# Gated delta attention and two MLPs: first loads, a solve moved one step earlier, and the second product two pairs behind

## The chip, the core and the metric

The kernel runs on one core of a Trainium2 chip. The metric is the device time of one execution in microseconds; all times here are in microseconds. A core has five engines that each run their own instructions in order: TensorE (PE in the rows; PEld are its weight loads), VectorE (DVE), ScalarE (ACT), GpSimd (POOL) and SyncE (SP, which here only issues DMA transfers). They wait for one another by semaphores.

## What is computed

Three parts run one after another; the output of each is the input of the next.

```python
# 1: attention with a state, per head, for t in 0..767 (4 batches, 8 heads, head dim 48)
k_n = k / (norm(k) + 1e-06)
y[t] = q[t] @ state
state += beta[t] * outer(k_n[t], v[t] - k_n[t] @ state)
# 2: 3072 tokens, 384 -> 2048 -> 384
h = maximum(x @ w_in, 0);  x = (h * h) @ w_out
# 3: 384 -> 768 -> 384
x = maximum(maximum(x @ w1, x @ w2), x @ w3) @ w_out2
```

The weights of parts 2 and 3 come as float64.

## The kernel before

**Chunks and systems.** The sequence is cut into 12 chunks of 64 positions, which are the 12 steps of the first two parts. Within a chunk the recurrence becomes a triangular system. `kkps` (L166) makes its matrix: K times K transposed (kk, L160, copied from PSUM by ScalarE at L175) and the masked product P with the queries (L176), two halves per chunk, stored to DRAM. `start32` (L252) loads kk again in another layout, M, with two chunks side by side on the 128 partitions (L262); `prep` (L222) copies the diagonal to ss (L224) and computes norms, a square root on ScalarE (L194) among them; `solve` (L238) eliminates with 61 VectorE instructions (L243, L245, L246); `finish32` stores the result xt (L278), which `attention` loads as xb. A solve so serves two chunks: `HALVED[g]` are chunks 2g and 2g+1.

**Attention of a chunk** (`attention`, L321) is a chain of small steps over two halves p (16 of the 32 batch-head pairs each): transposed blocks xT (L340), products pZ and pW, values scaled by the norms (`st0`, L361), `mm_u` (pU, L382), `st2` (pY, L395; the new state Sb, L404), `st3` (transposition pT, then xh, the high part on ScalarE, L419, and xl, the low part on VectorE, L420).

**First MLP of a chunk** (`moe_a`, L434). float32 operands are split in a high and a low part, and each product takes three matmuls. 16 blocks of 128 hidden units are taken in 8 pairs. For a pair, `s1` is 18 matmuls (L446), then ScalarE makes relu (L451), square (L452) and the high part gh (L453), VectorE the low part gl (L454), and `s2` is 18 matmuls with them (L465). The code runs s1 one pair ahead of s2. At the end, two copies xs (L476) leave for DRAM.

**Weights.** `convert` (L81) loads raw float64 bits (L87) and makes the two parts: an absolute value on ScalarE (L90), bit operations on VectorE (L93 to L98), the high part on ScalarE (L99), the low part on VectorE (L100). There are 16 pieces of w_in in the prologue, the first NE = 5 ahead of the first solve; 16 of w_out (8 in the prologue's end, the others in step 0); 12 of the second MLP's first weights in steps 9 to 11.

**Order.** The prologue makes kk of chunks 0 and 1, the first solve, attention(0) and w_in. Then `steps` (L480) runs twelve times moe_a(c) with other generators beside it, each advanced at its rate: attention(c + 1), kkps for a later pair of chunks and solve32 by the tables `KK` and `SOLVE` (step: pair of chunks). The code gives only an order of priority: a scheduler of the framework decides the final order on each engine, and extra order can be forced with `behind(i, j)`, which puts instruction i after j. Buffers of kk and P are pieces of two large tiles, big and buf, and in the prologue ksr. After the steps the second MLP runs (L637, L654).

## Time and profile before

| | us |
|---|---|
| median of 3 runs | 1062.96 (1060.36 to 1063.26) |
| the profiled execution | 1065.6 |
| its span | 1063.9 |
| PE busy | 933.4 (88%) |
| VectorE busy | 477.6 (45%) |
| ScalarE busy | 395.1 (37%) |
| chain that ended last | PE 73%, DVE 10%, DMA 10%, issue 3% |

The span is the time between the first and the last instruction of the profiled execution; the rest of its time lies around it. The chain that ended last is followed back from the last instruction, at each step to what released it. Step c begins here with the first matmul of moe_a(c) that reads xl: 111.1, 169.5, 243.9, 293.6, 350.5, 399.5, 458.1, 505.0, 562.2, 619.4, 671.2 and 716.2; the second MLP begins at 757.9.

### The profile page before, as it was taken

Reading aid. Unit: us, or ns where it says so; the run is one execution under the profiler, and the core shown is the slowest. Engines: PE = TensorE matmul, PEld = TensorE weight load, DVE = VectorE, ACT = ScalarE, POOL = GpSimd, SP = SyncE. Lnnn points to the kernel's source line nnn. Section 1 sums busy time; section 2 is a strip of 40 time slices with the busy share of each in tenths; the row PEclk is TensorE's granted clock in tenths of the full one; section 3 lists DMA queues with packets and bytes.
Section 4 is the critical chain, followed back from the end, with each engine's and each line's share of the span. In section 5 each row is a group of like instructions: output and inputs, shape, how many; then the busy total and the mean of one; then the engine's idle time right before and its main releaser. Section 6 shows DMA issues by size and latency. Waiting matters only on the chain.

```text
span 1063.9 us, 26753 instructions
## 1 busy us (share of the span) xinstructions
PE 933.4 (88%) x11706; PEld 856.9 (81%) x11706; DVE 477.6 (45%) x1057; ACT 395.1 (37%) x780; POOL 125.6 (12%) x200
## 2 busy tenths in 40 slices
PE   4004999959998999899988989998999999999998
PEld 4004898948997999799988979998888888888887
DVE  2799937547223841384257641227352323232221
ACT  2126653423443444344454444455431212121111
POOL 1323010130202020202020202000110000000000
PEclk8555898978999899999998989998999999999999
DMA  9954562552245134514452341104220100000001
GB/s 265 291 122 119 174 177 75 139 139 49 73 128 158 49 95 118 159 53 105 116 165 85 82 144 59 34 9 127 89 75 15 45 16 30 15 16 23 8 23 38
DMA packets 89333, 98.44 MB, mean 93 GB/s; under 512 B 49120, under 2 KB 66784, under 8 KB 89216
## 3 DMA queue, kind: packets, MB, share of 16 engines
q1 hardware_dynamic: 74624, 59.36, 20.3%
q0 software_dynamic: 10496, 31.60, 10.1%
q10 hardware_dynamic: 4096, 5.77, 1.6%
q8 instruction: 92, 1.51, 0.6%
q14 instruction: 25, 0.20, 0.1%
HBM read 71.53 MB, written 25.17 MB: 91 GB/s over the span
## 4 chain that ended last, share of the span: by engine, by line
PE 73%; DVE 10%; DMA 10%; issue 3%; ACT 3%; SPq 1%; POOL 1%; DVEq 0%; ACTq 0%; POOLq 0%
PE p L637 21%; PE p L446 17%; PE px L465 17%; PE po L654 7%; DMA buf<-kk 2%; PE pU L382 2%; DMA kk<-big 2%; DVE buf L243 2%; DVE buf L245 2%; DMA raw<-in_moe_w_dram 2%; PE pk L160 1%; PE pW L354 1%; PE pY L395 1%; PE pZ L344 1%; PE pA L372 1%
## 5 line engine op out<-in xcount | busy, mean ns | idle before, releaser
L465 PE MATMUL px<-gh,wout 128*128 128x256 f32 x1152 | 227.3, 296 | 22.3 <-ACT gh L453 22.3
L465 PEld LDWEIGHTS px<-gh,wout 128*128 128x128 f32 x1152 | 187.0, 200 | 26.2 <-ACT gh L453 23.6
L637 PE MATMUL p<-x_h,w 128*128 128x512 f32 x648 | 203.4, 395 | 0.0
L465 PE MATMUL px<-gl,wout 128*128 128x256 f32 x576 | 170.3, 296 | 5.9 <-DVE gl L454 5.8
L446 PE MATMUL p<-xh,win_h 128*128 128x256 f32 x576 | 169.9, 296 | 0.2
L446 PE MATMUL p<-xl,win_h 128*128 128x256 f32 x576 | 167.3, 294 | 0.0
L446 PE MATMUL p<-xh,win_l 128*128 128x256 f32 x576 | 166.3, 289 | 0.0
L454 DVE TENSOR_TENSOR gl<-p,gh 128x512 fp32r<-128x512 f32 x96 | 65.9, 687 | 175.9 <-ACT gh L453 175.4
L637 PEld LDWEIGHTS p<-x_h,w 128*128 128x128 f32 x648 | 121.6, 188 | 27.1
L637 PE MATMUL p<-x_l,w 128*128 128x512 f32 x324 | 128.1, 395 | 0.0
L451 ACT ACTIVATE gg<-p 128x512 f32<-128x512 f32 x96 | 57.1, 596 | 190.8 <-PE p L446 188.4
L465 PEld LDWEIGHTS px<-gl,wout 128*128 128x128 f32 x576 | 115.3, 200 | 8.4 <-DVE gl L454 7.9
L446 PEld LDWEIGHTS p<-xh,win_h 128*128 128x128 f32 x576 | 114.8, 199 | 1.9 <-ACT xh L419 0.7
L446 PEld LDWEIGHTS p<-xh,win_l 128*128 128x128 f32 x576 | 114.6, 199 | 0.0
L446 PEld LDWEIGHTS p<-xl,win_h 128*128 128x128 f32 x576 | 113.2, 198 | 1.6
L643 DVE TENSOR_TENSOR mx<-p,mx 128x512 f32<-128x512 f32 x36 | 24.9, 691 | 137.1 <-PE p L637 137.1
L637 PEld LDWEIGHTS p<-x_l,w 128*128 128x128 f32 x324 | 61.0, 188 | 14.6
L645 ACT CAST hh<-mx 128x512 fp32r<-128x512 f32 x36 | 22.3, 620 | 130.8 <-DVE mx L644 130.8
L245 DVE TENSOR_TENSOR buf<-buf 128x30 f32<-128x30 f32 (+9 forms) x180 | 59.5, 330 | 5.2
L243 DVE TENSOR_TENSOR buf<-buf 128x30 f32<-128x30 f32 (+9 forms) x180 | 59.2, 329 | 5.4
L452 ACT ACTIVATE p<-gg 128x512 f32<-128x512 f32 x96 | 57.6, 601 | 2.7
L453 ACT CAST gh<-p 128x512 fp32r<-128x512 f32 x96 | 56.1, 585 | 2.7
(132 smaller groups left out, 1362.0 us busy)
## 6 DMA issues: line engine op xcount, KB each, us to landing
kq<-in_kc_dram POOLq DMA_DIRECT2D x22, 448.0 KB, 4.1
raw<-in_moe_w_dram SPq DMA_DIRECT2D x18, 384.0 KB, 4.4
p<-p POOLq DMA_DIRECT2D x24, 256.0 KB, 3.3
raw<-in_moe_w_out_dram SPq DMA_DIRECT2D x13, 384.0 KB, 3.7
buf<-in_kc_dram SPq DMA_DIRECT2D x11, 448.0 KB, 3.8
big<-in_kc_dram SPq DMA_DIRECT2D x11, 448.0 KB, 4.3
v<-in_vt_dram POOLq DMA_DIRECT2D x24, 192.0 KB, 3.9
ktp<-in_kt_dram POOLq DMA_DIRECT2D x24, 192.0 KB, 3.4
```

The lines of the kernel that those rows point to most:

```text
L243: eng.tensor_tensor(out=tv, in0=M[:, 0:j, j].unsqueeze(2).broadcast_to([u, j, m]), in1=M[:, j, j + 1:n].unsqueeze(1).broadcast_to([u, j, m ...
L245: yield eng.tensor_tensor(out=M[:, 0:j, j + 1:n], in0=M[:, 0:j, j + 1:n], in1=tv, op=ALU.add)
L446: pe.matmul(p1[:, j], w[:, k, f], x[c][:, k], start=n == 0 and j == 0, stop=n == 8, skip_group_check=True)
L451: act.activation(out=gg, in_=p1, func=AF.Relu)
L452: act.activation(out=p1, in_=gg, func=AF.Square)
L453: act.copy(gh, p1)
L454: vec.tensor_sub(out=gl, in0=p1, in1=gh.bitcast(F32))
L465: pe.matmul(acc[m], w, x[:, j], start=f == 0 and i == 0 and m != 1, stop=f == NF - 1 and i == 2, skip_group_check=True)
L637: pe.matmul(p, w[i][:, k, fs], x[:, k], start=n == 0, stop=n == 8)
L643: vec.tensor_max(out=t, in0=ps[1], in1=t)
L645: act.copy(hh[:, f], t2)
L654: pe.matmul(po[:, 0:DM], x[:, f, js], w[:, f], start=i == 0, stop=i == 17)
```

## The change

1. **The start.** Four pieces of w_in instead of five are loaded first. The kk stores go out from SP instead of ScalarE; the stores of P of chunks 0 and 1 are later, on POOL. M of chunk 0 is loaded from POOL and of chunk 1 from SP. All other raw loads come behind the last load of M (`raw_after[:] = loaded`), and ss comes behind the fourth conversion (`prep_after`). The stores of xt go out from ScalarE and POOL.
2. **Chunk 0.** attention(0) takes both halves through each of its steps side by side, with tiles of their own.
3. **Chunks 2 and 3.** Their kk is made in the prologue, the mask product behind the first solve, instead of in step 0; their solve stands in step 0, behind the eighth conversion of w_out, instead of in step 1. attention(2) is no longer put off by 11 turns.
4. **The lag.** s2 stands two pairs behind s1 instead of one; relu works in place in PSUM, and gh and gl have three buffers.
5. **Second MLP's weights.** VectorE's part of the conversions in step 9 comes behind the last gl of step 8.

```diff
+LAG = 2
...
-        lo_eng.tensor_tensor(out=lo, in0=l.bitcast(F32), in1=hi.bitcast(F32), op=ALU.subtract)
+        parted.append(lo_eng.tensor_tensor(out=lo, in0=l.bitcast(F32), in1=hi.bitcast(F32), op=ALU.subtract).ins)
...
-    def kk_store(c, p, kk, dma):
-        return [dma.dma_start(kk_d[c][:, t, U2 * p:U2 * p + U2], kk[64 * t:64 * t + 64]).ins for t in range(2)]
-
-    def kkps(cs, ps_, dma=nc.sync):
+    def kk_store(c, p, kk):
+        for t in range(2):
+            nc.sync.dma_start(kk_d[c][:, t, U2 * p:U2 * p + U2], kk[64 * t:64 * t + 64])
+
+    def kkps(cs, ps_, late_p=None):
...
+            for i in mul_after:
+                behind(kk_ends[1], i)
             yield
-            stores = kk_store(c, p, ks[:, 0], dma)
-            for t in range(2):
-                o = 64 * t
-                stores.append(nc.sync.dma_start(p_d[c][o:o + 64, U2 * p:U2 * p + U2], ks[64 - o:128 - o, 1]).ins)
-            p_stored[:] = stores[2:]
+            kk_store(c, p, ks[:, 0])
+
+            def p_store(dma, c=c, p=p, ks=ks):
+                return [dma.dma_start(p_d[c][64 * t:64 * t + 64, U2 * p:U2 * p + U2], ks[64 - 64 * t:128 - 64 * t, 1]).ins for t in range(2)]
+
+            if late_p is None:
+                p_store(nc.sync)
+            else:
+                late_p.append(p_store)
...
+        i = vec.tensor_copy(ss, diagonal(M, n))
+        for j in prep_after:
+            behind(i.ins, j)
...
-                dma.dma_start(M[o:o + 32], units(kk_d[c][..., 32 * s:32 * s + 32], 32 * s, 32))
+                loaded[0] = dmas[i].dma_start(M[o:o + 32], units(kk_d[c][..., 32 * s:32 * s + 32], 32 * s, 32)).ins
...
-        for fs in ((st0, 0),), ((zz, k21),), ((ww, 0),), ((mm_u, 0),), ((st2, 0),), ((st0, 1), (st3, 0)), ((mm_u, 1),), ((st2, 1),), ((st3, 1),):
+        if c:
+            order = ((st0, 0),), ((zz, k21),), ((ww, 0),), ((mm_u, 0),), ((st2, 0),), ((st0, 1), (st3, 0)), ((mm_u, 1),), ((st2, 1),), ((st3, 1),)
+        else:
+            order = ((st0, 0), (st0, 1)), ((zz, k21),), ((ww, 0),), ((mm_u, 0), (mm_u, 1)), ((st2, 0), (st2, 1)), ((st3, 0), (st3, 1))
+        for fs in order:
...
-            gg = gp.tile([128, 2, TB], F32, name="gg", tag="gg")
-            gh = gp.tile([128, 2, TB], F32R, name="gh", tag="gh")
-            gl = gp.tile([128, 2, TB], F32R, name="gl", tag="gl")
-            act.activation(out=gg, in_=p1, func=AF.Relu)
-            act.activation(out=p1, in_=gg, func=AF.Square)
+            gh = gp.tile([128, 2, TB], F32R, name="gh", tag="gh", bufs=LAG + 1)
+            gl = gp.tile([128, 2, TB], F32R, name="gl", tag="gl", bufs=LAG + 1)
+            act.activation(out=p1, in_=p1, func=AF.Relu)
+            act.activation(out=p1, in_=p1, func=AF.Square)
             act.copy(gh, p1)
-            vec.tensor_sub(out=gl, in0=p1, in1=gh.bitcast(F32))
+            last_gl[0] = vec.tensor_sub(out=gl, in0=p1, in1=gh.bitcast(F32)).ins
...
-            if fp:
-                s2(fp - 1)
+            if fp >= LAG:
+                s2(fp - LAG)
...
-        s2(NF // 2 - 1)
+        for fp in range(NF // 2 - LAG, NF // 2):
+            s2(fp)
+            if fp < NF // 2 - 1:
+                yield
         for i, n in enumerate((2, 1)):
-            xs = gp.tile([128, 2, TB], F32, name="xs", tag="gg")
+            xs = gp.tile([128, 2, TB], F32, name="xs", tag="xs", bufs=1)
...
+                for j in solve_after:
+                    behind(i.ins, j)
...
-        drain(kkps(HALVED[0], (p1, at), act))
-        NE = 5
-        raw_done = list(p_stored)
+        ps_stores = []
+        drain(kkps(HALVED[0], (p1, at), ps_stores))
+
+        NE = 4
         after[:], abs_after[:] = kk_ends[1:], kk_ends[0:1]
         for f in range(NE):
             load_win(f, vec, nc.sync)
-        raw_after[:] = raw_done
-        drain(solve32(0, pool))
-        x_after.append(selected[0])
-        drain(attention(0))
-        x_after.clear()
+        prep_after.append(parted[-1])
+        first_solve = solve32(0, (pool, nc.sync), (act, pool))
+        next(first_solve)
+        prep_after.clear()
+        raw_after[:] = loaded
+        stores = [i for f in ps_stores for i in f(pool)]
+        for i in stores:
+            behind(i, selected[0])
+        drain(first_solve)
+        solved.append(ops[-1])
+        x_after.append(stores[-1])
         after[:], abs_after[:] = ops[-1:], normed[0:1]
         for f in range(NE, NF):
             load_win(f, vec, nc.sync)
+
+        mul_after.append(solved[0])
+        kc_after.append(raws[-1])
+        drain(kkps(HALVED[1], (p1, at)))
+        mul_after.clear()
+        kc_after.clear()
+        drain(attention(0))
...
-        KK, SOLVE = {0: 1, 1: 2, 3: 3, 5: 4, 7: 5}, {1: 1, 2: 2, 4: 3, 6: 4, 8: 5}
+        KK, SOLVE = {1: 2, 3: 3, 5: 4, 7: 5}, {0: 1, 2: 2, 4: 3, 6: 4, 8: 5}
...
-                extra.append((1.3, later(11, attention(c + 1))) if c == 1 else (9 / 15.0, attention(c + 1)))
+                extra.append((9 / 15.0, attention(c + 1)))
...
-                extra.append((8.0 if c == 1 else 5.0, solve32(SOLVE[c])))
+                extra.append((5.0, later(45, solve32(SOLVE[c])) if c == 0 else solve32(SOLVE[c])))
+            if c == 0:
+                solve_after.append(parted[NF + 7])
+            if c == 1:
+                solve_after.clear()
             if c == 9:
+                after[:] = last_gl
```

How the order moves is shown at three places. The names are the tiles: kk_93 and kk_94 are kk of chunks 0 and 1 in DRAM, p_105 and p_106 their P, raw, rawp, big and buf take raw weights.

On SP, in the prologue behind the first loads, before:

```order
L87 DMA raw<-in_moe_w_in_dram 128x3x256 x3
L87 DMA big<-in_moe_w_in_dram 128x3x256 x2
L259 DMA b_409<-in_beta_dram 64x32 x2
L149 DMA buf<-in_kc_dram 112x1024
L181 DMA p_105<-buf 64x512 x2
L149 DMA big<-in_kc_dram 112x1024
L181 DMA p_105<-big 64x512 x2
L181 DMA p_106<-ksr_194 64x512 x2
L181 DMA p_106<-ksr_195 64x512 x2
L87 DMA big<-in_moe_w_in_dram 128x3x256
```

and with the change:

```order
L89 DMA raw<-in_moe_w_in_dram 128x3x256 x3
L89 DMA big<-in_moe_w_in_dram 128x3x256
L273 DMA b_392<-in_beta_dram 64x32 x2
L169 DMA kk_93<-buf 64x512 x2
L169 DMA kk_93<-big 64x512 x2
L169 DMA kk_94<-ksr_194 64x512 x2
L169 DMA kk_94<-ksr_195 64x512 x2
L276 DMA buf<-kk_94 32x32x32 x2
L89 DMA big<-in_moe_w_in_dram 128x3x256 x2
```

The stores of kk and a load of M now stand on this queue ahead of the second lot of weights; the loads of keys for chunks 2 and 3 and the stores of P have left it.

On VectorE, from the last product of the first solve (L246, then L260) on, before:

```order
L246 TENSOR_TENSOR buf<-buf,a_408 128x1024
L361 TENSOR_TENSOR r<-v,normT 128x384 x2
L93 TENSOR_SCALAR cvt<-cvt 128x384 x2
L96 TENSOR_SCALAR cvt<-cvt 128x384 x2
L97 SCALAR_TENSOR_TENSOR big<-big,cvt 128x384
L97 SCALAR_TENSOR_TENSOR buf<-buf,cvt 128x384
```

and with the change:

```order
L260 TENSOR_TENSOR buf<-buf,a_391 128x1024
L95 TENSOR_SCALAR cvt<-cvt 128x384 x2
L182 TENSOR_TENSOR buf<-pq,mask 128x512
L182 TENSOR_TENSOR big<-pq,mask 128x512
L378 TENSOR_TENSOR r<-v,normT 128x384
L182 TENSOR_TENSOR ksr_194<-pq,mask 128x512
L378 TENSOR_TENSOR r_798<-v,normT 128x384
L98 TENSOR_SCALAR cvt<-cvt 128x384 x2
L182 TENSOR_TENSOR ksr_195<-pq,mask 128x512
```

The four mask products of chunks 2 and 3 stand right behind the solve, between the two halves of attention(0) and the conversions.

On ScalarE, at the end of step 3 (the last pair's relu is L451, then L474), before:

```order
L383 COPY u<-pU 128x384
L175 COPY big<-pk 128x512
L451 ACTIVATE gg<-p_4200 128x512
L194 ACTIVATE s_4354<-ss 128x32
L452 ACTIVATE p_4200<-gg 128x512
L453 CAST gh<-p_4200 128x512
L410 COPY yy<-pY 64x4x48 x4
L476 COPY xs<-px 128x512
L476 COPY xs<-px 128x256
L419 CAST xh<-pT 128x3x128
```

and with the change:

```order
L400 COPY u<-pU 128x384
L181 COPY big<-pk 128x512
L474 ACTIVATE p_4151<-p_4151 128x512
L475 ACTIVATE p_4151<-p_4151 128x512
L476 CAST gh<-p_4151 128x512
L430 COPY yy<-pY 64x4x48 x4
L206 ACTIVATE s_4321<-ss 128x32
L502 COPY xs<-px 128x512
L439 CAST xh<-pT 128x3x128
```

The square root (L194, then L206) has moved from ahead of the last pair's square to behind its gh and behind yy, ahead of xs and xh.

## Rows read from the trace of the kernel before

**Rows 1.** The page's 40 slices of the span (26.6 us each), in tenths.

```profile
PE   4004999959998999899988989998999999999998
PEclk8555898978999899999998989998999999999999
```

**Rows 2.** Windows by stretch: length, busy us (instructions) of each engine, clock, DMA share.

```profile
core 0: us, PE busy (x) PEld busy (x) DVE busy (x) ACT busy (x) POOL busy (x), PEclk, DMA share, GB/s
0.00:37.10 37.10, 12.94 (x304) 12.48 (x304) 13.01 (x30) 8.79 (x16) 6.00 (x18) 0.72 0.97 253
65.60:169.50 103.90, 72.33 (x1393) 67.31 (x1393) 79.03 (x192) 58.75 (x123) 22.63 (x31) 0.75 0.53 146
169.50:243.90 74.40, 59.42 (x973) 56.09 (x972) 45.50 (x121) 24.18 (x50) 12.19 (x19) 0.84 0.45 117
243.90:293.60 49.70, 49.64 (x772) 47.29 (x771) 22.00 (x51) 21.52 (x42) 8.42 (x14) 0.95 0.26 71
293.60:350.50 56.90, 52.22 (x1001) 49.60 (x999) 19.13 (x43) 24.41 (x51) 9.65 (x15) 0.97 0.48 134
350.50:399.50 49.00, 48.21 (x750) 45.99 (x742) 28.28 (x69) 21.49 (x42) 8.42 (x14) 0.97 0.27 74
399.50:458.10 58.60, 53.64 (x1002) 50.76 (x998) 19.43 (x44) 24.40 (x51) 9.65 (x15) 0.94 0.46 132
458.10:505.00 46.90, 46.84 (x747) 44.69 (x744) 27.89 (x67) 21.59 (x42) 8.39 (x14) 1.00 0.29 76
505.00:562.20 57.20, 52.71 (x1011) 49.97 (x1007) 22.79 (x51) 28.54 (x59) 9.65 (x15) 0.97 0.49 139
562.20:619.40 57.20, 51.24 (x700) 47.89 (x694) 38.75 (x102) 26.21 (x52) 8.43 (x14) 0.91 0.36 99
619.40:671.20 51.80, 49.13 (x790) 46.61 (x782) 15.63 (x30) 23.24 (x47) 8.43 (x14) 0.97 0.29 89
...
757.90:1063.90 306.00, 302.40 (x1406) 258.22 (x1404) 89.13 (x130) 67.27 (x117) 6.85 (x6) 1.00 0.10 34
```

**Rows 3.** Timeline of VectorE in the start: start, us, form, [idle before, releaser].

```profile
30.12 0.55 DVE L100 TENSOR_TENSOR win_l<-big,win_h 128x384 fp32r<-128x384 f32 x1
...
37.12 0.19 DVE L224 COPY ss<-buf 128x32 f32<-128x32 f32 x1 [4.23 <-DMA buf<-kk]
```

**Rows 4.** Timeline of ScalarE: the last kk copy of chunks 0 and 1.

```profile
21.04 0.58 ACT L175 COPY ksr<-pk 128x512 f32<-128x512 f32 x1 [1.17 <-issue]
21.52 0.99 ACT L90 ACTIVATE cvt<-raw 128x384 f32<-128x384 f32 x2
```

**Rows 5.** Timeline of POOL: the second issue of M loads.

```profile
27.39 1.56 POOL L262 DMA_DIRECT2D buf<-kk  x2 [2.26 <-issue]
```

**Rows 6.** Timeline of TensorE in the start: kk of chunk 1.

```profile
16.70 0.37 PE L160 MATMUL pq<-kct 48*64 48x64 f32 x1 [3.90 <-issue]
```

**Rows 7.** Timeline at the end of step 3, ScalarE, VectorE, then TensorE.

```profile
332.30 0.59 ACT L175 COPY big<-pk 128x512 f32<-128x512 f32 x1
...
341.62 0.19 DVE L224 COPY ss<-buf 128x32 f32<-128x32 f32 x1 [3.34 <-DMA buf<-kk]
...
341.84 0.23 ACT L194 ACTIVATE s<-ss 128x32 f32<-128x32 f32 x1 [4.80 <-DVE ss L224]
...
343.23 0.50 PE L465 MATMUL px<-gh,wout 128*128 128x256 f32 x2 [3.40 <-ACT gh L453]
```

**Rows 8.** Timeline of TensorE in step 1: attention of chunk 2.

```profile
229.58 1.95 PE L382 MATMUL pU<-r,xb 64*64 64x48 f32 x32 [7.93 <-DVE r L375]
```

**Rows 9.** Timeline of VectorE: first solve's ends, second solve's end, then xT.

```profile
42.44 0.15 DVE L243 TENSOR_TENSOR buf<-buf 128x30 f32<-128x30 f32 x1
...
64.35 1.23 DVE L246 TENSOR_TENSOR buf<-buf,a 128x1024 f32<-128x1024 f32 x1
...
198.25 1.23 DVE L246 TENSOR_TENSOR buf<-buf,a 128x1024 f32<-128x1024 f32 x1
...
208.72 0.71 DVE L340 STREAM_TRANSPOSE xT<-xb 128x512 f32<-128x512 f32 x1 [3.37 <-DMA xb<-xt]
```

**Rows 10.** Timeline of ScalarE in step 8: a conversion of w3.

```profile
569.01 0.54 ACT L90 ACTIVATE cvt<-raw 128x384 f32<-128x384 f32 x1 [3.15 <-DMA raw<-in_moe_w_dram]
```

More of the change, by code (lines that the diff above doesn't have):

```diff
@@ L68, in delta_moe @@
     after, abs_after, raw_after, x_after, raws = [], [], [], [], []
-    NR, NRP = 3, 9
+    parted, last_gl = [], [None]
+    NR = 3
     def raw_tile(shape):
@@ L148, in kkp_load @@
         kcs[c, p] = k
-        nc.sync.dma_start(k, two(kc, c, p).rearrange("p b q t s -> p (b q) t s"))
+        i = nc.sync.dma_start(k, two(kc, c, p).rearrange("p b q t s -> p (b q) t s"))
+        for j in kc_after:
+            behind(i.ins, j)
     def kk_matmul(c, p, ps_):
@@ L215, in strict @@
         eng.memset(diagonal(M, n), 1.0)
-    selected = [None]
+    selected, loaded, prep_after = [None], [None], []
     def diagonal(M, n):
@@ L223, in prep @@
         ss = pool_.tile([128, n], F32, name="ss", tag="ss", bufs=1)[0:u]
-        vec.tensor_copy(ss, diagonal(M, n))
+        i = vec.tensor_copy(ss, diagonal(M, n))
+        for j in prep_after:
+            behind(i.ins, j)
         nm, r = weighted(ss, n, u, bt, a, pool_)
@@ L318, in delta_moe @@
     xh, xl = {}, {}
-    ops, normed = [], []
+    ops, normed, solved, solve_after = [], [], [], []
     def attention(c):
@@ L329, in fresh @@
         def fresh(name, p, i, shape):
-            t = att.tile(shape, F32, name=name, tag=name)
+            if name == "r" and p and not c:
+                t = pkp.tile(shape, F32, name="r1", tag="r1")
+            else:
+                t = att.tile(shape, F32, name=name, tag=name, bufs=1 if name == "r" else 2)
             tiles[c, p][i] = t
@@ L362, in st0 @@
             if c < 2:
-                behind(i.ins, ops[-1])
+                behind(i.ins, solved[0])
             if not c:
@@ L389, in st2 @@
             if not c:
-                pY = ps_y.tile([128, U2, D], F32, name="pY", tag="y")
+                pY = (ps_at if p else ps_y).tile([128, U2, D], F32, name="pY", tag="at" if p else "y")
             if c < NC - 1:
@@ L406, in st2 @@
                     vec.tensor_copy(sv, pD)
-            yy[p] = att.tile([128, Q, 2, D], F32, name="yy", tag="yy", bufs=1)
+            if p and not c:
+                yy[p] = pkp.tile([128, Q, 2, D], F32, name="yy1", tag="yy1")
+            else:
+                yy[p] = att.tile([128, Q, 2, D], F32, name="yy", tag="yy", bufs=1)
             for i in range(2):
@@ L425, in attention @@
         load_att(c, 1)
-        for fs in ((st0, 0),), ((zz, k21),), ((ww, 0),), ((mm_u, 0),), ((st2, 0),), ((st0, 1), (st3, 0)), ((mm_u, 1),), ((st2, 1),), ((st3, 1),):
+        if c:
+            order = ((st0, 0),), ((zz, k21),), ((ww, 0),), ((mm_u, 0),), ((st2, 0),), ((st0, 1), (st3, 0)), ((mm_u, 1),), ((st2, 1),), ((st3, 1),)
+        else:
+            order = ((st0, 0), (st0, 1)), ((zz, k21),), ((ww, 0),), ((mm_u, 0), (mm_u, 1)), ((st2, 0), (st2, 1)), ((st3, 0), (st3, 1))
+        for fs in order:
             for f, p in fs:
                 f(p)
-                if f is mm_u and p and c + 1 < NC:
+                if f is (mm_u if c else st2) and p and c + 1 < NC:
                     load_att(c + 1, 0)
@@ L546, in delta_moe, with solve32 @@
             behind(pool.memset(t_, 0.0).ins, i_mask.ins)
-        def solve32(g, *dma):
-            M, a, norm = start32(g, *dma)
+        def solve32(g, load=(nc.sync, nc.sync), store=(nc.sync, nc.sync)):
+            M, a, norm = start32(g, load)
             normed.append(norm())
@@ L552, in solve32 @@
             for i in solve(vec, M, 32, 64 * len(HALVED[g]), a, tmp32):
+                for j in solve_after:
+                    behind(i.ins, j)
                 ops.append(i.ins)
                 yield
-            finish32(g, M, *dma)
+            finish32(g, M, store)
         def later(n, g):
@@ L613, in delta_moe @@
                 wb = ctx.enter_context(tc.tile_pool(name="wb", bufs=1, side="right", reuse_waits="tile"))
+                after.clear()
                 extra.append((0.5, w3load((2,))))
```

9 lines of the change are left out of this document (5 added, 4 removed).

## The prediction

> **What bounds the kernel now.** I read the page's slices of the span first. TensorE is busy in nearly every slice except the first few and those around step 1, and its clock is low there too [rows 1]. So I cut the trace at the starts of the steps, and at the end of the first solve (65.6). The reader should compare the span of a stretch with TensorE's busy time in it [rows 2]. The last stretch, the second MLP, is 306.0 long with 302.4 busy: the change does not touch it, and there is nothing to win. The even steps 4 and 6 (49.0, 46.9) are almost pure TensorE work. Steps 3, 5 and 7 (56.9, 58.6, 57.2) have 52.2 to 53.6 of it: about 5 more because they compute K times K transposed (kk) for two later chunks, and the rest is waiting. Three stretches are far from TensorE's work: the start to the first solve's end, where TensorE has 12.9 in the first 37.1; from there to step 1, with 72.3 busy in 103.9 at a clock of 0.75, and VectorE at 79.0; and step 1, with 59.4 in 74.4 at 0.84.
>
> Then I asked in each of these stretches which wait ends last. In the start it is the reload of kk: VectorE's first instruction of the preparation, the copy of the diagonal to ss, stands at 37.12 after 4.23 of waiting for M from DRAM [rows 3]. In step 1 it is attention(2), whose products wait for one another (7.93 in one place, [rows 8]) because the solve that they need ended only at 199.5 [rows 9]. At the end of step 3 it is ScalarE, where the square root of the norms waits 4.80 for M and holds up the square of the last pair; TensorE then waits 3.40 [rows 7]. In step 8 it is a conversion on ScalarE that waits for raw weights [rows 10].
>
> **Term A, the start: -9.** The last kk copy starts at 21.04, after 1.17 in which ScalarE issued its own stores, and the conversions' absolute values start behind it at 21.52 [rows 4]. The fourth conversion ends at 30.12 + 0.55 = 30.7 on VectorE [rows 3], so four take 9.2 from there, with a fifth mixed in. The stores now leave from SP, and the copy can follow TensorE (which comes back at 16.70, [rows 6]) by about 3, at 19.5: the fourth conversion then ends at 28.0 or so. [...] Now the bulk loads wait for the M loads. At the end of step 3, where the rings are quieter, copy to ss takes 341.6 - 332.3 = 9.3, store, load and all [rows 7]: 19.5 + 9.3 = 28.8. Both give about 28, against 37.1. [...] I take 9, since the row of step 3 is the same chain. What is late next is the fourth conversion, which stands in front of ss by the new order.
>
> TensorE's pause of 3.90 has "issue" as its cause, that is, no semaphore [rows 6]. [...] No row here ties the pause to a load, and I leave it as it is.
>
> **Term B, first solve to step 1: -1.** VectorE has 79.0 of work in these 103.9 [rows 2]. The change puts the second solve in here: it takes 23 (the first one began at 42.44 and ended at 64.35 + 1.23 = 65.6, [rows 9]), while its preparation stood before 169.5 already. That is 102: the engine would be full from end to end, and step 1 starts when the last xl is made. The kk of chunks 2 and 3 only moves within the stretch: TensorE, with 72 of 104, has room. Attention(0) with both halves side by side shortens a chain that stood beside the conversions, so I cost it at nothing; its cover is VectorE's queue, where the conversions stand between its steps. The weights' reloads can cost 1 to 4, since their buffers are read late. If VectorE fills every gap, 102 less overlap of neighbours gives -4; if 10 of its 25 idle stay, +8. I take -1, nearest to full, since the solve has no partner on another engine and fills any gap.
>
> **Term C, steps 1 and 2: -17.5.** Step 1 no longer contains a solve, so attention(2) is no longer held to its end, and step 1 becomes a kk step like 3, 5 and 7: their mean is 57.6 [rows 2]. Step 2 is like 4 and 6: 49 at most. Together 106.6 against 74.4 + 49.7 = 124.1. Bounds: -24, if step 1 has none of the others' boundary wait; -10, if its attention still has half its waits.
>
> **Term D, steps 3 to 7: -5.** The lag of two takes the 3.40 out of the place where it is now: when the last pair's gh is late, two second products of earlier pairs, not one, stand ahead of the one that needs it. But M lands as late as before, and the square root that waits for it now stands ahead of the copies xs and xh, which the next step needs. In step 3 the first product with xl came 350.5 - 341.6 = 8.9 after M [rows 2, 7]. That chain loses the square and gh, two passes of about 0.6 (the copy of the same shape took 0.59, [rows 7]), 1.2 in all; the preparation on VectorE comes ahead of Sb and xl and can give it back. So a kk step wins nothing if the chain stays, and 3.4 if TensorE's whole wait is filled; I take 1.7, the middle and near the 1.2, in each of steps 3, 5 and 7. Bounds for the three: nothing, and -12 (3.4 and a little more for gl behind it).
>
> **Term E, steps 8 and 9: -9.** Step 8 becomes an even step (49) when the conversions of w3 leave it: 57.2 - 49 = 8 [rows 2]. Step 9 was 51.8 and now holds what step 8 held, but there the waits on ScalarE ([rows 10], 3.15) have a lag of two pairs as cover: 51 at most, 1 won. Bounds: -3 (the waits merely move), -13 (both steps at 48).
>
> **Term F, steps 10 and 11: -1** (0 to -3): small waits that the lag covers. Removing the tile gg and relu in place change no count.
>
> **Sum**: -9 - 1 - 17.5 - 5 - 9 - 1 = -42.5. The span goes from 1063.9 to 1021.4, the profiled execution from 1065.6 to 1023.1. The median of the runs, 1062.96, lies 2.6 below the profiled execution; so I forecast **1020.5**, and as this case's own range, with the terms' errors partly cancelling, 1008 to 1033. Chance 0.55.
>
> **The rivals.** (1) The lag covers the whole boundary of the kk steps. For it: TensorE's busy time there is only 5 above that of an even step. Then each kk step is 48 + 5.3 = 53.3 against 57.6, 4.3 in four steps, 17 against the 5 of D: 1008.5. Against: the square root still waits for M ahead of xh. Chance 0.14. (2) The gain of the start is given back: raw loads held back until M has landed come too late for conversions 5 to 16, and VectorE idles behind the solve, in the stretch where it has 79.0 of work in 103.9 already [rows 2]. A is lost: 1029.5. Against: the solve gives them 37 to land. Chance 0.12. (3) The wait of step 1 moves. The solve, pushed behind a conversion of w_out, ends around the start of step 1, and from its end to xT is 208.72 - 199.48 = 9.2 [rows 9]; then attention(2) is late again and C is nothing: 1038. Chance 0.13. (4) Slower. [...] Chance 0.03. [...] (5) The change does not do what it says, because the scheduler's order gives back in one stretch what it wins in another: 1063, chance 0.03.
>
> **How the numbers follow.** The range runs from 1000 (rival 1 with the lower bound of C) to 1040 (just above rival 3); outside lie rivals 4 and 5, the far half of 3 and the lower end of 1: under 2 in 10. A difference of 0.3%, 3 us, is about what a measurement of this kernel can tell from none. Faster by more: 0.95, all of the forecast and rivals 1 to 3 and a part of 5; within it 0.02; slower 0.03.
>
> **What would show it.** A: ss near 28 instead of 37.12. B: step 1 starts about 10 earlier than 169.5, VectorE without idle from the solve on. C: step 1 near 57 with no wait of more than 4 in attention(2); the second solve over before step 1. D: no wait of 3.4 before the last pair's second product, but one before the next step's first. E: step 8 near 49. Wrong would be: ss above 34, a first product of step 1 after 172, step 1 above 65, a low clock through whole steps, or kk steps below 54.

## The result, and the profile after

The changed kernel takes a median of 1028.8 us (4 runs, 1025.28 to 1031.07) beside 1061.66 (4 runs) of the kernel before: a ratio of 0.969, 95% interval 0.9664 to 0.9715. The forecast was 1020.5, with 1000 to 1040 as its range: the direction and the range are right, and the gain of 33 is smaller than the 42 expected. The profiled execution took 1031.07 and its span is 1029.4, against 1063.9. The page's slices, to be read beside [rows 1]; a slice is now 25.7 long:

```profile
PE   4034699989998999899999999999999999999998
PEclk8555699989999999989999989999999999999999
```

The 5 in slice 9, in step 1, has gone. Slices 2 to 5 read 0, 3, 4 and 6, where they read 0, 0, 4 and 9 before; step 0 begins in the fifth. The windows by stretch, columns as in [rows 2]; the first two are from the first solve's end to step 0 and step 0, then steps 1 to 4, 8, 9 and 11:

```profile
55.60:113.70 58.10, 26.92 (x630) 24.36 (x623) 45.37 (x115) 26.72 (x56) 13.39 (x19) 0.53 0.60 161
113.70:171.30 57.60, 51.46 (x737) 48.95 (x736) 49.27 (x129) 31.02 (x66) 5.79 (x10) 0.90 0.39 129
171.30:227.60 56.30, 51.05 (x998) 48.37 (x998) 19.11 (x43) 24.71 (x51) 12.32 (x19) 0.97 0.56 150
227.60:276.30 48.70, 48.70 (x745) 46.41 (x745) 28.62 (x70) 21.54 (x42) 8.45 (x14) 0.96 0.28 74
276.30:331.40 55.10, 50.90 (x1000) 48.52 (x999) 16.99 (x34) 24.22 (x51) 9.69 (x15) 0.99 0.48 134
331.40:380.60 49.20, 49.16 (x743) 47.05 (x743) 30.17 (x78) 21.54 (x42) 8.46 (x14) 0.94 0.28 79
540.40:589.20 48.80, 48.80 (x742) 46.71 (x742) 35.20 (x91) 23.27 (x45) 8.46 (x14) 0.95 0.28 73
589.20:641.20 52.00, 49.51 (x744) 47.17 (x742) 31.71 (x67) 30.00 (x62) 8.44 (x14) 0.93 0.48 150
687.40:723.20 35.80, 34.98 (x287) 34.36 (x286) 22.98 (x48) 21.34 (x41) 0.00 (x0) 1.00 0.31 99
```

In the kernel before, the same view of the first two stretches and of step 11:

```profile
65.60:111.10 45.50, 17.48 (x379) 15.13 (x379) 44.47 (x112) 26.22 (x55) 15.35 (x20) 0.50 0.50 134
111.10:169.50 58.40, 54.85 (x1018) 52.19 (x1015) 34.57 (x82) 32.53 (x68) 7.29 (x11) 0.94 0.55 156
716.20:757.90 41.70, 37.27 (x287) 36.57 (x286) 22.63 (x47) 20.47 (x40) 0.00 (x0) 0.92 0.28 86
```

The reader should compare VectorE, the third pair of numbers, with the length. Before, it had 44.5 of work in the 45.5 ahead of step 0, so it was full. Now it has 45.4 in 58.1: almost the same work, with 12.7 of standing. In step 0 itself it is the other way round: 49.3 instead of 34.6 of work in the same length, so most of the second solve fitted there for nothing.

By the prediction's terms, from one profiled execution each (starts of steps as before: 113.7, 171.3, 227.6, 276.3, 331.4, 380.6, 437.7, 487.0, 540.4, 589.2, 641.2, 687.4, and 723.2 for the second MLP; the first solve ends at 54.37 + 1.23 = 55.6):

| term | stretch | before | after | moved | forecast |
|---|---|---|---|---|---|
| A | start to end of first solve | 65.6 | 55.6 | -10.0 | -9 |
| B | from there to step 1 | 103.9 | 115.7 | +11.8 | -1 |
| C | steps 1 and 2 | 124.1 | 105.0 | -19.1 | -17.5 |
| D | steps 3 to 7 | 268.6 | 264.1 | -4.5 | -5 |
| E | steps 8 and 9 | 109.0 | 100.8 | -8.2 | -9 |
| F | steps 10 and 11 | 86.7 | 82.0 | -4.7 | -1 |
| | second MLP | 306.0 | 306.2 | +0.2 | 0 |
| | span | 1063.9 | 1029.4 | -34.5 | -42.5 |

B is the miss: it ate all of A. Where VectorE stands is in its timeline (start, length, form, idle before and its releaser), which answers to [rows 3] and [rows 9]:

```profile
27.37 0.18 DVE L236 COPY ss<-buf 128x32 f32<-128x32 f32 x1
...
54.37 1.23 DVE L260 TENSOR_TENSOR buf<-buf,a 128x1024 f32<-128x1024 f32 x1
...
56.84 0.69 DVE L182 TENSOR_TENSOR buf<-pq,mask 128x512 f32<-128x512 f32 x1 [0.71 <-PE pq L164]
58.57 0.69 DVE L182 TENSOR_TENSOR big<-pq,mask 128x512 f32<-128x512 f32 x1 [1.03 <-PE pq L164]
...
64.98 0.69 DVE L182 TENSOR_TENSOR ksr<-pq,mask 128x512 f32<-128x512 f32 x1 [5.26 <-PE pq L164]
...
70.05 0.81 DVE L95 TENSOR_SCALAR cvt<-cvt 128x384 f32<-128x384 f32 x2 [0.90 <-ACT cvt L92]
...
87.41 0.19 DVE L236 COPY ss<-buf 128x32 f32<-128x32 f32 x1 [4.65 <-DMA buf<-kk]
```

The first ss does not wait any more (27.37, with no idle before it, instead of 37.12 after 4.23). Then VectorE stands 7.0 in front of three mask products of chunks 2 and 3, 0.9 behind a late ScalarE, and 4.65 in front of the second ss, whose M is not there: 12.6 in all. The mask products wait for TensorE, and TensorE for the keys. First TensorE's row, then the two of SP's queue that issued the raw weights and, behind them, the first keys:

```profile
54.77 0.37 PE L164 MATMUL pk<-buf 48*64 48x64 f32 x2 [24.27 <-DMA buf<-in_kc_dram]
```

```profile
24.98 10.28 SPq L89 DMA_DIRECT2D rawp<-in_moe_w_in_dram  x9
35.36 1.52 SPq L151 DMA_DIRECT2D buf<-in_kc_dram  x1
```

The keys of chunks 2 and 3 are issued at 35.4, behind nine loads of raw weights, and the first of them is used at 54.8: 19 from issue to use, where TensorE has waited 24. The transfers that SP issued between 22.3 and 40.0 landed in the order of their issue: the last of the nine raw loads at 52.8, and the first keys behind them at 54.6.

### The profile page after: what moved, and what is told of

Its sections match the earlier page's. It is cut to its first block, busy times and chain, and to the rows that moved or that the text cites. A ratio compares the mean times of both kernels' runs of the same rounds, so it can differ in the third digit from the quotient of the medians.

```text
span 1029.4 us, 26724 instructions
## 1 busy us (share of the span) xinstructions
PE 925.8 (90%) x11706; PEld 851.9 (83%) x11706; DVE 476.0 (46%) x1057; ACT 394.3 (38%) x780; POOL 125.5 (12%) x204
## 4 chain that ended last, share of the span: by engine, by line
PE 74%; DMA 9%; DVE 8%; issue 5%; SPq 2%; ACT 1%; POOL 1%; ACTq 0%; DVEq 0%; POOLq 0%
PE p L686 22%; PE p L470 18%; PE px L488 15%; PE po L703 7%; DMA kct<-in_kc_dram 2%; PE pU L399 2%; DMA buf<-kk 2%; DMA kk<-big 2%; PE pW L371 1%; PE pY L412 1%; PE pA L389 1%; SPq L89 1%; PE pZ L361 1%; DMA buf<-in_kc_dram 1%; PE pk L164 1%
## 5 line engine op out<-in xcount | busy, mean ns | idle before, releaser
L488 PE MATMUL px<-gh,wout 128*128 128x256 f32 x1152 | 219.6, 289 | 7.7 <-ACT gh L476 7.7
L488 PEld LDWEIGHTS px<-gh,wout 128*128 128x128 f32 x1152 | 180.5, 192 | 10.6 <-ACT gh L476 8.1
L470 PE MATMUL p<-xh,win_h 128*128 128x256 f32 x576 | 174.0, 303 | 3.5 <-DVE gl L477 2.6
L470 PE MATMUL p<-xl,win_h 128*128 128x256 f32 x576 | 170.1, 299 | 4.9 <-DVE xl L440 4.9
L470 PE MATMUL p<-xh,win_l 128*128 128x256 f32 x576 | 169.3, 295 | 0.0
L488 PE MATMUL px<-gl,wout 128*128 128x256 f32 x576 | 163.2, 283 | 0.0
L470 PEld LDWEIGHTS p<-xl,win_h 128*128 128x128 f32 x576 | 116.5, 204 | 6.6 <-DVE xl L440 5.6
L470 PEld LDWEIGHTS p<-xh,win_l 128*128 128x128 f32 x576 | 117.4, 204 | 0.1
L488 PEld LDWEIGHTS px<-gl,wout 128*128 128x128 f32 x576 | 110.9, 192 | 0.0
L474 ACT ACTIVATE p<-p 128x512 f32<-128x512 f32 x96 | 55.9, 583 | 134.8 <-PE p L470 133.3
L694 ACT CAST hh<-mx 128x512 fp32r<-128x512 f32 x36 | 22.3, 620 | 128.9 <-DVE mx L693 128.9
L476 ACT CAST gh<-p 128x512 fp32r<-128x512 f32 x96 | 56.3, 587 | 2.6
L475 ACT ACTIVATE p<-p 128x512 f32<-128x512 f32 x96 | 55.9, 582 | 2.7
```

What stands on the lines that cost most here:

```text
L470: pe.matmul(p1[:, j], w[:, k, f], x[c][:, k], start=n == 0 and j == 0, stop=n == 8, skip_group_check=True)
L474: act.activation(out=p1, in_=p1, func=AF.Relu)
L475: act.activation(out=p1, in_=p1, func=AF.Square)
L476: act.copy(gh, p1)
L488: pe.matmul(acc[m], w, x[:, j], start=f == 0 and i == 0 and m != 1, stop=f == NF - 1 and i == 2, skip_group_check=True)
L694: act.copy(hh[:, f], t2)
```

## The experiments

All start from the changed kernel, unless said otherwise. The table has, of each profiled execution, the first solve's end, the start of step 0, the length of the steps and the span; the medians and ratios (to the kernel before, on the same chip) stand with each experiment.

| run | solve ends | step 0 at | step 0 | 1 | 2 | 3 to 7 | 8, 9 | 10, 11 | span |
|---|---|---|---|---|---|---|---|---|---|
| before | 65.6 | 111.1 | 58.4 | 74.4 | 49.7 | 268.6 | 109.0 | 86.7 | 1063.9 |
| after | 55.6 | 113.7 | 57.6 | 56.3 | 48.7 | 264.1 | 100.8 | 82.0 | 1029.4 |
| 1 keys early | 55.7 | 115.7 | 52.5 | 60.1 | 47.5 | 265.0 | 100.6 | 81.5 | 1029.2 |
| 2 xt on POOL | 55.8 | 114.4 | 55.4 | 62.5 | 48.9 | 265.8 | 100.9 | 81.3 | 1035.8 |
| 3 both | 55.1 | 115.7 | 53.5 | 61.5 | 47.7 | 264.1 | 101.5 | 81.5 | 1031.8 |
| 4 lag of one | 55.3 | 114.7 | 57.4 | 63.0 | 47.0 | 260.2 | 101.9 | 82.8 | 1033.1 |
| 5 second ss late | 55.1 | 107.8 | 58.3 | 57.9 | 48.4 | 266.1 | 101.9 | 81.1 | 1027.7 |
| 6 all three | 54.5 | 104.3 | 54.3 | 61.0 | 48.4 | 263.4 | 99.2 | 82.1 | 1019.0 |
| 7 masks late | 56.1 | 110.3 | 56.6 | 59.6 | 49.0 | 267.3 | 101.9 | 81.1 | 1032.1 |
| 8 part 3 undone | 56.3 | 96.7 | 66.2 | 74.7 | 49.6 | 265.6 | 99.8 | 81.9 | 1040.6 |
| 9 boundaries free | 55.9 | 107.7 | 54.5 | 55.2 | 47.6 | 246.0 | 101.3 | 81.8 | 1000.6 |
| 10 and attention(2) later | 56.3 | 103.9 | 53.7 | 62.1 | 48.9 | 246.1 | 100.8 | 81.9 | 1003.7 |
| 11 part 5 undone | 55.2 | 113.1 | 58.7 | 62.3 | 48.6 | 268.7 | 102.9 | 81.1 | 1041.6 |
| 12 part 2 undone | 55.7 | 117.6 | 55.4 | 61.4 | 47.7 | 261.0 | 100.9 | 81.1 | 1031.2 |

**1. The keys ahead of the raw weights.**

```diff
-        kc_after.append(raws[-1])
-        drain(kkps(HALVED[1], (p1, at)))
+        kc_after.append(loaded[0])
+        second = kkps(HALVED[1], (p1, at))
+        next(second)
+        raw_after[:] = loaded + kc_loads[-4:]
```

(This stands ahead of the loads of the rest of w_in, and `kc_loads` are the loads of the keys; the rest of `second` comes behind them.)

> The change lost 12 of its gain between the first solve's end (55.8) and step 0 (113.7). Theory 1: VectorE stands at the mask products of chunks 2 and 3, whose keys were loaded behind all raw weights and landed only at 54.6 to 60.1; with the keys loaded ahead of the raw weights the waits of 0.7, 1.0 and 5.3 there and the 4.65 for the second M go, step 0 starts near 102 and the time is 1016 to 1019. Theory 2: attention(0) paces this stretch by xb, which landed at 78.4 because the xt stores of chunk 0 on ScalarE left only at 67.9; they leave from the same queue here, so 1024 to 1028. Theory 3: VectorE simply has that much work: 1028.

Measured: 1034.17 (1030.89 to 1037.58), ratio 0.9722 (0.9692 to 0.9752). Nothing won. VectorE's timeline shows where the 7.0 went:

```profile
55.60 0.68 DVE L183 TENSOR_TENSOR buf<-pq,mask 128x512 f32<-128x512 f32 x1
57.04 0.67 DVE L183 TENSOR_TENSOR big<-pq,mask 128x512 f32<-128x512 f32 x1
57.63 1.27 DVE L183 TENSOR_TENSOR ksr<-pq,mask 128x512 f32<-128x512 f32 x2
...
70.90 0.80 DVE L95 TENSOR_SCALAR cvt<-cvt 128x384 f32<-128x384 f32 x2 [8.63 <-ACT cvt L92]
...
85.75 0.19 DVE L237 COPY ss<-buf 128x32 f32<-128x32 f32 x1 [3.65 <-issue]
```

The mask products no longer wait, as theory 1 wanted, and yet step 0 is not earlier. The stand of 8.63 is now behind ScalarE, which in its own order issues the xt stores of chunk 0 ahead of its conversions; they leave only at 68.8:

```profile
68.82 1.40 ACTq L293 DMA_DIRECT2D xt<-buf  x2
```

The semaphores in the trace tell why. In this program the transfers of SP and ScalarE take turns at eight semaphores that report their landing, and an issue first waits until the transfer that had its semaphore before has landed: in the changed kernel's trace none of 276 such issues leaves ahead of that landing. Ahead of the first of these stores that was a load of keys that SP had issued at 59.9: it landed at 68.72, and the store left at 68.82. In the changed kernel such a load landed at 67.76, and the store left at 67.86.

**2. The xt stores of chunk 0 on POOL.**

```diff
-        first_solve = solve32(0, (pool, nc.sync), (act, pool))
+        first_solve = solve32(0, (pool, nc.sync), (pool, pool))
```

> Only the xt stores of chunk 0 move from ScalarE to POOL, as they were in the kernel before. Theory 1 (the mask products wait for the keys): 1027 to 1029, VectorE's wait of 5.3 stays. Theory 2 (attention(0) waits for xb): xb lands near 70 instead of 78.4, step 0 starts 5 to 8 earlier, 1021 to 1024. Theory 3: 1028.

Measured: 1038.22 (1034.44 to 1040.66), ratio 0.9758 (0.9723 to 0.9793). The products pZ with xb began at 72.8 instead of 78.1, so theory 2's link is right, but step 0 did not move (114.4): a wait that others hide. The 6 more in the span are step 1, to which experiment 6 comes.

**3. Both.**

> Keys ahead of the raw weights and the xt stores on POOL. Theory 1: as with the keys alone, 1016 to 1019. Theory 2: as with the stores alone or better, 1016 to 1022. If both waits stand side by side and each alone hides the other's removal: the two alone give under 4 each and this one 10 to 12, so 1016 to 1018. Theory 3: 1028.

Measured: 1034.38 (1031.47 to 1035.39), ratio 0.972 (0.9695 to 0.9744). One single stand of VectorE is left between the solve and step 0:

```profile
87.34 0.19 DVE L237 COPY ss<-buf 128x32 f32<-128x32 f32 x1 [13.38 <-DMA buf<-kk]
```

All three theories, as I had put them, fail here. VectorE works through what it has sooner and then stands 13.4 in front of the second ss, until M of chunks 2 and 3 lands: this ss stands between 85.8 and 88.4 in the changed kernel and in experiments 1 to 4. The earlier waits had only used up time that would have been spent here.

M is late with the keys early, too, and that is SP's order again. In experiment 1, ScalarE's last copy of kk ends at 44.1, but the stores of kk leave between 53.7 and 69.0, among loads of weights, and the last load of M at 79.3, behind the stores of P:

```profile
43.47 0.59 ACT L182 COPY ksr<-pk 128x512 f32<-128x512 f32 x1 [3.17 <-PE pk L165]
53.69 1.30 SPq L170 DMA_DIRECT2D kk<-buf  x2
64.31 4.64 SPq L170 DMA_DIRECT2D kk<-ksr  x4
79.30 0.38 SPq L277 DMA_DIRECT2D buf<-kk  x1
```

The first of these stores left at 53.69 because the raw load that had its semaphore before landed at 53.62. Whether M comes sooner with these stores on another queue was not tried.

**4. The lag of one.**

```diff
-LAG = 2
+LAG = 1
```

> The second product one pair behind the first, as before, all else as changed. If terms D, E and F (17.4 measured in steps 3 to 11) come from the lag: kk steps back to 57.6, step 9 back by 2 or more, in all 8 to 12 more than the change, 1037 to 1041. Rival: the waits only moved to the first product of the next step, and the lag itself is worth under 3: 1029 to 1032.

Measured: 1035.15 (1034.85 to 1041.63), ratio 0.9746 (0.9712 to 0.9779); the interval just touches the change's. But the stages contradict the reason that I gave: steps 3 to 7 are 260.2, 4 shorter than with the lag of two, steps 8 to 11 1.9 longer; the time is lost in step 1. At the end of step 3 TensorE waits at the same places with a lag of two and of one. With two:

```profile
328.45 0.28 PE L249 MATMUL pt<-ident,nm 128*32 128x128 f32 x1 [3.24 <-DVE nm L211]
331.44 0.58 PE L470 MATMUL p<-xl,win_h 128*128 128x256 f32 x1 [0.60 <-DVE xl L440]
```

and with one:

```profile
334.03 0.28 PE L249 MATMUL pt<-ident,nm 128*32 128x128 f32 x1 [3.28 <-DVE nm L211]
337.11 0.58 PE L470 MATMUL p<-xl,win_h 128*128 128x256 f32 x1 [0.54 <-DVE xl L440]
```

Neither waits 3.4 at the last pair's second product as in [rows 7]; both wait for nm, the norms of the next solve, which TensorE transposes ahead of the next step's products. In both, the new order has the square root behind the last gh.

At the ends of steps 1 and 5 it is otherwise. There, with a lag of one, TensorE does wait at a second product of the last pair, as in the kernel before, and with two it does not:

```profile
227.35 0.80 PE L488 MATMUL px<-gh,wout 128*128 128x256 f32 x2 [3.42 <-ACT gh L476]
435.81 0.58 PE L488 MATMUL px<-gl,wout 128*128 128x256 f32 x1 [3.60 <-DVE gl L477]
```

So the lag of two does keep that wait away. It does not make the steps shorter, because other waits, as those for nm above, take its place.

**5. The second ss behind the last conversion of w_in.**

```diff
             if c == 0:
                 solve_after.append(parted[NF + 7])
+                prep_after.append(parted[NF - 1])
```

> Only the preparation of the second solve moves on VectorE: its copy to ss comes behind the last conversion of w_in. In the last three runs VectorE lost 12 to 13 between the solves whatever was moved, and each time the second ss was the last to wait (4.7, 3.7, 4.9, 13.4): M of chunks 2 and 3 lands at 85 to 87 in all of them. Theory 4: VectorE, in order, is held at this ss, and nothing else needs it early; here the wait of 4.65 goes, the 7.0 at the mask products stay: step 0 starts 4 to 5 earlier, 1024 to 1026 beside 1029. Theory 3 (VectorE has that much work): 1029.

Measured: 1032.49 (1029.4 to 1033.35), ratio 0.9718 (0.969 to 0.9747). The wait for M went, and step 0 starts 5.9 earlier; the steps gave back 4 of this in small pieces, and the median is not told apart from the change's.

**6. Keys early, xt on POOL and the second ss late.** The three edits together.

> Keys ahead of the raw weights, xt stores on POOL, and the second preparation behind the last conversion of w_in. Theory 4: no wait of VectorE over 1 is left between the first solve and step 0, step 0 starts at 102 to 104 instead of 113.7, and the time is 1016 to 1020 beside 1029. Theory 5: attention(0) has a chain of its own of about 35 from xb to xl, so step 0 starts at 71 + 35 = 106, 1021 to 1023. Theory 3: 1029.

Measured: 1024.66 (1020.69 to 1026.73), ratio 0.9645 (0.961 to 0.968); the span is 1019.0. The window between solve and step 0:

```profile
54.50:104.30 49.80, 19.15 (x395) 17.07 (x395) 47.34 (x121) 24.47 (x53) 14.56 (x21) 0.50 0.70 190
```

VectorE has 47.3 of work in 49.8. Step 0 starts at 104.3, 9.4 earlier than with the change, so theory 3 is out. The start is theory 4's but for 0.3, though one wait of over 1 is left: 1.82 at the second ss, which comes at 85.8 here and still meets M late. A chain of attention(0) (theory 5: 106) is not excluded as the next bound, though VectorE has only 2.5 of idle time left. The median is 5 above theory 4's, and that is step 1, which gives 4.7 back. There VectorE stands at xT of chunk 2, in front of a gl, because the second solve ended at 156.9 and its result needs the way through DRAM, 7.4 from there to xT; then TensorE stands:

```profile
155.68 1.23 DVE L261 TENSOR_TENSOR buf<-buf,a 128x1024 f32<-128x1024 f32 x1
...
164.26 0.71 DVE L358 STREAM_TRANSPOSE xT<-xb 128x512 f32<-128x512 f32 x1 [6.21 <-DMA xb<-xt]
```

```profile
167.64 0.36 PE L471 MATMUL p<-xh,win_h 128*128 128x256 f32 x1 [3.75 <-DVE gl L478]
```

In the changed kernel's trace a gl stood ahead of this xT, and the waits were 0.88 and 0.39; that is a part of why its step 1 is 56.3 and that of experiments 2, 3 and 6 over 60. In experiment 6, TensorE stands 2.4 longer over the step, and its matmuls are 2.2 longer busy, at a clock of 0.95 instead of 0.97.

**7. The masks later instead of the keys earlier.**

```diff
-        mul_after.append(solved[0])
+        mul_after.append(parted[NE + 5])
```

(with the second ss late and xt on POOL)

> The keys stay behind the raw weights; instead the mask products of chunks 2 and 3 come later on VectorE (behind conversion 9 of w_in), the second preparation behind the last conversion, and the xt stores of chunk 0 on POOL. Theory 4: the same 1016 to 1020 as with the keys early, since what costs is VectorE standing, not the late keys. If the late keys themselves cost (second solve's end): step 1 is longer, 1022 to 1026. Theory 3: 1029.

Measured: 1031.57 (1029.27 to 1033.79), ratio 0.9715 (0.9686 to 0.9744), span 1032.1: against theory 4 in this form. The masks no longer held VectorE, but it stood 8.77 behind ScalarE at 69.07, and ScalarE's copies of kk still waited for the late keys: they stood between 59.2 and 68.0, the last after 4.78 of waiting for TensorE. The late keys cost here, too, only through another engine that met them in its order.

**8. Part 3 undone alone.**

```diff
-        KK, SOLVE = {1: 2, 3: 3, 5: 4, 7: 5}, {0: 1, 2: 2, 4: 3, 6: 4, 8: 5}
+        KK, SOLVE = {0: 1, 1: 2, 3: 3, 5: 4, 7: 5}, {1: 1, 2: 2, 4: 3, 6: 4, 8: 5}
```

(with the calls in the prologue and step 0 as before)

> Part 3 undone alone: kk of chunks 2 and 3 in step 0 and their solve in step 1, attention(2) put off, as before; first loads, attention(0) side by side and lag as changed. The prediction's sum: term C (19.1 measured) is lost, and the 12.6 that part 3 cost ahead of step 0 come back: step 0 starts near 101, 1034 to 1038 beside 1029. If the 12.6 are not part 3's: step 0 starts at 113 and the time is 1046 to 1050.

Measured: 1041.03 (1039.47 to 1044.51), ratio 0.9806 (0.9768 to 0.9844). The windows of the stretch before step 0, of step 0 and of step 1:

```profile
56.30:96.70 40.40, 18.03 (x398) 15.94 (x399) 39.45 (x99) 23.82 (x52) 12.72 (x19) 0.54 0.39 93
96.70:162.90 66.20, 57.57 (x986) 54.42 (x986) 37.54 (x89) 33.99 (x73) 6.70 (x11) 0.89 0.63 183
162.90:237.60 74.70, 59.68 (x982) 56.23 (x982) 47.44 (x124) 24.50 (x51) 12.23 (x19) 0.84 0.44 113
```

Without part 3, VectorE is full ahead of step 0 (39.5 in 40.4) and step 0 starts at 96.7: this is what part 3 costs there, 17.0. The xt stores on ScalarE are not late here either, so that part of the price came with part 3's loads of keys:

```profile
56.29 0.97 ACTq L292 DMA_DIRECT2D xt<-buf  x2
```

Step 0 is 8.6 longer without it, step 1 18.4 longer, nearly as before. So part 3 is worth 11.2 net in the spans, and 9.4 of its price goes in experiment 6. The other 7.6 are mostly work that stands ahead of step 0 now: VectorE has 47.3 there in experiment 6 beside 39.5 here, among it four mask products (2.7) and the second preparation (3.4). The median lies above the first expectation by 3 and below the second.

**9. No preparation at the boundaries.** Experiment 6, and for the later solves:

```diff
+            prep_after[:] = last_xl[0:1]
```

(`last_xl` is the last xl that st3 made, that is, the low part of the next step's input)

> The last version (keys ahead of the raw weights, xt stores on POOL, second preparation behind the last conversion of w_in), and for the later solves the copy to ss behind the last xl of the next step's input, so that the square root, the norms and their transposition on TensorE no longer stand at the boundary. With the lag of one, the kk steps were as short as with two, and at the end of step 3 TensorE waited 3.24 for the transposition of nm, and 0.6 for xl, in both. Theory 6: what costs a kk step is not the second product but whatever stands behind M in the engines' orders; steps 1, 3, 5 and 7 become 2.5 to 3.5 shorter each (step 3 at 52.5 to 53.5), 10 to 13 together: 1012 to 1016 beside 1025 for the last version. Rival: the later preparation ends the solve later, and the even steps lengthen by as much: 1022 to 1026.

Measured: 999.43 (6 runs, 995.03 to 1004.34), ratio 0.9411 (0.9371 to 0.9451), span 1000.6. This beats both kernels, and by more than theory 6 asked: steps 3 to 7 take 246.0 instead of 263.4 in experiment 6 and 264.1 in the changed kernel. Steps 3, 4 and 5 here:

```profile
265.00:315.20 50.20, 49.81 (x975) 47.97 (x975) 12.51 (x21) 23.39 (x46) 8.42 (x14) 1.00 0.56 150
315.20:362.90 47.70, 47.70 (x770) 45.38 (x768) 34.22 (x90) 22.24 (x47) 9.68 (x15) 1.00 0.30 79
362.90:413.10 50.20, 49.81 (x975) 47.97 (x975) 12.70 (x22) 23.71 (x47) 8.43 (x15) 1.00 0.56 150
```

The kk step is 50.2, and TensorE is busy 49.8 of it, at a clock of 1.00. Some 25 small matmuls have moved from it into the step behind it, but steps 3 and 4 together take 97.9 beside 104.3 in the changed kernel. The square root, the norms and their transposition, which waited for M between two steps, were nearly the whole of the boundary. Step 1 still has its wait at a gl behind xT, 3.83, and is 55.2: this order costs about 5 there. Step 0 starts 3.4 later than in experiment 6, though nothing ahead of it was edited.

**10. attention(2) three turns later.**

```diff
-                extra.append((9 / 15.0, attention(c + 1)))
+                extra.append((9 / 15.0, later(3, attention(c + 1)) if c == 1 else attention(c + 1)))
```

> As the run before it, and attention(2) begins three turns later in step 1. In the version with all three moves VectorE stood 6.21 at xT of chunk 2, with gl behind it, and TensorE 3.75 behind that; step 1 was 61.0 instead of 56.3. If this wait is the whole of it: step 1 is 3 to 5 shorter than in the run before, 1009 to 1013. If the later attention makes the end of step 1 late by as much: no difference, 1012 to 1016.

Measured: 1009.74 (1005.41 to 1013.92), ratio 0.9519 (0.9467 to 0.9571): slower than experiment 9. Step 1 is 62.1 instead of 55.2. VectorE still stands 6.26 at xT, so the edit did not take that wait away, and TensorE waits 3.05 in the later attention near the end of the step: that is the second case, only dearer.

**11. Part 5 undone alone.**

```diff
-                after[:] = last_gl
+                pass
```

> The changed kernel without part 5 alone: VectorE's part of the conversions of w3 in step 9 is not held behind the last gl of step 8. If term E (8.2 measured in steps 8 and 9) is part 5's: step 8 is near 57 again and the time 1035 to 1038 beside 1029. If the lag covers the conversions in step 8: 1028 to 1031. The lag of one left step 8 at 47.7, which speaks for part 5.

Measured: 1047.3 (1043.28 to 1049.46), ratio 0.9855 (0.9808 to 0.9902), span 1041.6, 12.2 more than the changed kernel's and over both expectations. Only 2.1 of these lie in steps 8 and 9: step 8 is 54.2 instead of 48.8, and step 9 48.6 instead of 52.0. 11.0 lie ahead of step 8, 6.0 of them in step 1 and 4.6 in steps 3 to 7, where the edit does nothing by itself: the scheduler gave the engines another order, on VectorE from step 0 on. So part 5 moves 5.4 out of step 8 and puts 3.4 into step 9, and this run can't price it by its total.

**12. Part 2 undone alone.**

```diff
-        if c:
+        if True:
             order = ((st0, 0),), ((zz, k21),), ...
```

> The changed kernel without part 2 alone: attention(0) takes its halves one after the other, as before. I costed this part at nothing, because VectorE's queue paces the stretch: 1028 to 1031 beside 1029. Theory 5 (attention(0) is a chain of its own that paces step 0): its second half adds the 8 to 10 that two more rounds between the engines cost: 1036 to 1039.

Measured: 1033.02 (1032.9 to 1033.96), ratio 0.9727 (0.9683 to 0.977). Between the two expectations: step 0 starts 3.9 later, and 2.2 of that are given back in step 0. By this stretch side by side is worth 1.7, and not the 8 to 10 of a chain that sets the pace; by the ratio it is not told apart from nothing.

## Why the prediction was right, and where it was not

**A was right** in size (10.0 against 9) and by its reason: M is there when the fourth conversion ends, and that conversion is what ss follows now. M's loads took at most 3.8 from issue to landing, from SP and from POOL, where the last had taken 8.8. The end of step 3, from which the forecast's 9.3 comes, was quieter: a DMA share of 0.68 from 332.3 to 341.6, beside 0.95 from 15.0 to 28.2 (the trace shows queues, not rings). In the kernel before, M left from POOL and the bulk loads of weights from SP, on two different queues of the trace (q0 and q1); how far the one held up the other is not shown, and part 1 was not undone alone. TensorE's pause in the start stayed (3.30 instead of 3.90). Over the experiments, which have the same first loads, it lies between 1.4 and 3.8, so its change is not put down to part 1; what it waits for is not shown.

**B failed**, by 12.8, and with it the forecast by 8 (C and F gave 5 back). Its sum took VectorE as full from the solve on, with 102 of work. By the windows above it had 94.6 of work in 115.7 and stood for 21.1, of these 12.7 ahead of step 0. The step of it that fell is the sentence that the kk of chunks 2 and 3 "only moves within the stretch: TensorE, with 72 of 104, has room". I counted the instructions and TensorE's room, and not the queue that the move put the keys behind, nor what stands behind a waiting mask product on VectorE, which was full in that stretch. The other half of B was right: the solve of 23, most of it in step 0, cost nothing there (57.6 against 58.4), as it filled idle time. Part 3 moved the mask products and the second preparation to a place where VectorE had no idle time to speak of (44.5 of work in 45.5), and its loads of keys held up the xt stores that part 1 had put on ScalarE; each of the three waited for a transfer. The order that I quoted showed the mask products right behind the solve; I read it and did not price it.

**C was right** (19.1 against 17.5), and experiment 8 shows that it is part 3's: with the solve in step 1, step 1 is 74.7. Rival 3 is real but smaller than I made it: where xT stands ahead of a gl, step 1 is 60 to 63 (experiments 1 to 4, 6 and 12), and not 74, and experiment 9 puts this order at about 5. Experiments 7 and 11 have a step 1 of 60 and 62 without this order.

**D was right in size (4.5 against 5) and wrong in its reason.** I put it down to the lag, with 1.7 in each of steps 3, 5 and 7. They are 1.8, 1.5 and 3.8 shorter, and steps 4 and 6 together 2.6 longer, so that the balance is near the forecast by luck; step 7, at 53.4, even falls below the 54 that the prediction named as a sign of being wrong. With a lag of one, steps 3 to 7 are not longer (260.2): the lag keeps the wait away from the second product, but the wait comes back elsewhere. At the end of step 3 the place of [rows 7] is free with either lag, because the new order has the square root behind the last gh in both; the wait for M then stands in front of the transposition of nm. This part of the order was quoted, and the prediction says that the wait stays in another place, which it did; what it did not see is that the lag is not needed for it there. Which edit moved the square root (relu in place, the separate tile for xs, or the scheduler's new start) was not tried.

**E** (8.2 against 9): step 8 is 8.4 shorter, as forecast, and 5.4 of it come back without part 5; the lag does not replace it there. Step 9 did not win its 1. Over the two steps, though, either of the two parts alone leaves 102 to 103 (experiments 4 and 11) against 109.0 before and 100.8 with both; a kernel with neither was not run.

**F** (4.7 against 1) was a term that I took as small waits without looking. Step 11 of the kernel before has one of 4.08, with a conversion that waits for raw weights on ScalarE ahead of it, as in [rows 10], and a clock of 0.50 behind it:

```profile
719.64 0.55 ACT L90 ACTIVATE cvt<-raw 128x384 f32<-128x384 f32 x1 [2.50 <-DMA raw<-in_moe_w_dram]
724.27 0.79 PE L465 MATMUL px<-gh,wout 128*128 128x256 f32 x2 [4.08 <-ACT gh L453]
```

Step 11 went from 41.7 to 35.8, and it is 37.6 with a lag of one: the lag has a part in it, the rest was not tried.

**Rival 1** (the boundary covered) did not come about by the lag, but experiment 9 reached it by taking the preparation away from there: 50.2 where I had set the floor at 53.3. My floor was TensorE's busy time before, which held matmuls at a clock below 1.00 (0.94 to 0.97 in steps 3, 5 and 7) and those that experiment 9 moves into the next step. **Rival 2** named the right place, the loads behind the held-back raw weights, but the wrong load: the conversions had their weights, the keys came late. **Rival 4** (slower) did not happen: TensorE's clock was 0.90 in step 0, where it had 0.94 before, and 0.97 in step 1.
